# Attention in 256-query strips with the score matmuls in groups of 12, on one Trainium2 core

## The chip, the cores and the metric

The kernel runs on 1 core of one Trainium2 chip. The metric is the device time of one execution in microseconds (us). Executions of one kernel agree within about 0.3%; each was run several times and the median is quoted. Where a ratio is given, it compares the fast runs of two kernels of the same rounds, with a 95% interval, so it is not quite the ratio of the medians.

Engine names in the profile: PE is TensorE's matmuls, PEld its weight loads, DVE is VectorE, ACT is ScalarE, POOL is GpSimd, SP is SyncE.

## The reference

Attention without a softmax over 8 batches of 3008 positions, then an MLP on the 24064 rows:

```python
scores = (1.0 / S) * np.matmul(z, z.transpose(0, 2, 1))   # z: (8, 3008, 64)
attn = np.maximum(scores, 0.0) ** 2
x = (u * np.matmul(attn, v)).reshape(B * S, D)            # u, v: (8, 3008, 256)
h = x @ w_in                                              # (256, 2048)
out = (h * (1.0 / (1.0 + np.exp(-1.702 * h)))) @ w_out    # (2048, 256)
```

## The kernel before

The sequence is padded to 24 blocks of 128. The contraction of a score matmul is only 64 long, so the kernel keeps `z` transposed twice in `ZT`: in partitions 0 to 63 and again in 64 to 127. Two score matmuls (two blocks of keys) can then use the two halves of the array's rows at once (in the trace below they start 3 ns apart). Each strip of 512 queries runs over 12 pairs of key blocks ("units"):

```python
ISUP = 512                                   # queries in a strip
ps_sc: bufs=2, each [128, 2, 512] f32        # 2 score tiles = 4 PSUM banks
ps_o:  bufs=2, each [128, 4, 256] f32        # 2 outputs O  = 4 PSUM banks
...
for gk in range(B * NIT + DPIPE):            # one unit per turn
    ... # casts of V for the next batch, alternating VectorE and ScalarE
    for g in range(2):                       # 2 score matmuls, one per half of the rows
        j = 2 * jp + g
        h0 = g * DQK                         # DQK = 64
        pe.matmul(sc[:, g, :], ZT[h0:h0 + DQK, j * P:(j + 1) * P],
                  ZT[h0:h0 + DQK, isup * ISUP:(isup + 1) * ISUP], start=True, stop=True)
    # unit gk - 1: r = relu(sc), every 5th on VectorE, else on ScalarE
    # unit gk - 1: ap_ = r * r, every 4th on GpSimd, else on VectorE
    # unit gk - 6: 8 value matmuls of 256 columns, O += ap_.T @ V16
    ...
    # end of a strip: X = O * ru on VectorE (ru holds the rows of u)
```

The second copy of `z` in `ZT` is made by a DMA from the first. The order of the instructions on every engine is chosen by the framework's scheduler. `X` goes to DRAM (`xdram`) and comes back transposed (`XT`) for the MLP stage, which the change does not touch.

## Time and profile before

| | before |
|---|---|
| time, median | 1516.7 us |
| first value matmul | 35.2 us |
| last value matmul | 821.5 us |
| one unit in the steady stage | 1.302 us |
| batches 2 to 6, each | 96.7 to 98.9 us |

A batch is measured from its first score matmul to the next batch's (for the last one, to the last value matmul). The times of the table come from the start times in the trace.

The page first: busy time and share of the span, then the chain of work that ended last.

```profile
PE 1449.0 (96%) x10464; PEld 916.0 (61%) x10464; DVE 1124.2 (74%) x1117; ACT 891.2 (59%) x869; POOL 284.7 (19%) x152
...
PE 73%; DVE 2%; ACT 1%; issue 1%; DMA 0%; SPq 0%; ACTq 0%
PE hg L299 23%; PE yps L324 22%; PE O L260 21%; PE sc L225 7%; ACT r L239 1%; DVE X L269 0%; DVE r L237 0%; DMA xdram<-X 0%; PE ztp L132 0%; DVE V_4421 L188 0%; DVE GT L307 0%; DVE V_5575 L188 0%; ACT tsg L306 0%; ACT V_6729 L190 0%; DVE ap__7938 L245 0%
```

TensorE bounds the kernel. But a busy PE is not a PE at its peak, because the ends of matmuls in the profile are modelled: value matmuls are recorded with 272 ns each and start 109 ns apart. The timeline of PE (start in us, duration, engine, line, operation, tiles, shapes, count) shows the steady stage:

```profile
416.34 0.39 PE L225 MATMUL sc<-ZT 64*128 64x512 f16 x2
416.66 1.05 PE L260 MATMUL O<-V_2113,ap__4472 128*128 128x256 f16 x8
417.64 0.39 PE L225 MATMUL sc<-ZT 64*128 64x512 f16 x2
417.96 1.05 PE L260 MATMUL O<-V_2113,ap__4488 128*128 128x256 f16 x8
```

From one pair of scores to the next is 1.30 us. `64*128` on the score lines is the part of the array in use: 64 active rows of the 128 that the value matmuls show. The start times of the single instructions show what the 1.30 us hold (start in us, engine, tile):

```
416.133 PE    O<-V,ap     last of 8 value matmuls, these start 109 ns apart
416.333 PEld  <-ZT        200 ns later: 109 of streaming, 91 of nothing
416.338 PE    sc<-ZT      half 0 of the rows
416.341 PE    sc<-ZT      half 1 of the rows, 3 ns later
416.655 PEld  <-ap        314 ns later: 216 of streaming, 98 of nothing
416.659 PE    O<-V,ap     first of the next 8
```

The 216 ns are what matmuls of 512 columns take elsewhere in this trace: those of the MLP stage start 215 to 216 ns apart. (The prediction below took about 213, and so 101 for the second gap.) So 8 x 109 ns of value matmuls, one stream of 216 ns for both scores, and about 0.2 us in which nothing streams, for each of 576 units.

Last, what PE waited for (us in total, times, longest), and the windows view of the undisturbed middle of attention. Its columns are: stretch, length, then for PE, PEld, DVE, ACT and POOL the busy time with the number of instructions, the granted clock, the DMA share and GB/s.

```profile
PE sc L225 <- DMA ZT<-ZT: 17.0, 1, 17.0
PE ztp L132 <- DVE zst_90 L110: 11.2, 1, 11.2
PE sc L225 <- DVE r L237: 10.6, 11, 2.4
PE hg L299 <- DVE GT L307: 8.7, 2, 7.9
PE sc L225 <- ACT r L239: 5.7, 5, 4.1
```

```profile
core 0: us, PE busy (x) PEld busy (x) DVE busy (x) ACT busy (x) POOL busy (x), PEclk, DMA share, GB/s
200.00:700.00 500.00, 490.12 (x3816) 302.69 (x3815) 389.22 (x405) 323.88 (x313) 179.25 (x92) 1.00 0.26 74
```

The first scores wait 17 us for the DMA that makes the second copy of `z`; after that there is little waiting. VectorE is busy 389 of 500 us, 78%.

### The profile page before, as it was taken

How to read it: one execution, taken by the hardware profiler on the slowest of the kernel's cores; microseconds unless marked ns; L12 is line 12 of the kernel's file. 1: busy time of each engine (PE TensorE's matmuls, PEld its weight loads, DVE VectorE, ACT ScalarE, POOL GpSimd, SP SyncE). 2: the span in 40 equal slices, each digit the busy share in tenths (PEclk: the TensorE clock that was granted, in tenths of full speed). 3: DMA queues.
4: the chain of work that ended last, by engine and by line, in shares of the span. 5: the costliest groups of instructions: out<-in, count | busy, mean ns of one | idle time of the engine just before them, and what ended most of it. 6: DMA issues, size and time to landing. Idle time of an engine off the chain costs nothing.

```text
span 1513.0 us, 24662 instructions
## 1 busy us (share of the span) xinstructions
PE 1449.0 (96%) x10464; PEld 916.0 (61%) x10464; DVE 1124.2 (74%) x1117; ACT 891.2 (59%) x869; POOL 284.7 (19%) x152
## 2 busy tenths in 40 slices
PE   2999999999999999999997999999999999999998
PEld 1565565665656666666665566666666666666666
DVE  3877678778777777777775877777777777777775
ACT  2765566666666676666664665555555655655553
POOL 0333333333333333333432000000000000000000
PEclk9999999999999999999999999999999999999999
DMA  9924325025142121211201112112111121121111
GB/s 307 261 70 115 96 58 164 29 58 164 48 132 67 42 70 34 82 33 43 78 29 54 36 56 64 49 57 59 51 59 49 57 63 49 56 63 50 57 44 48
DMA packets 175422, 113.66 MB, mean 75 GB/s; under 512 B 77776, under 2 KB 174032, under 8 KB 175056
## 3 DMA queue, kind: packets, MB, share of 16 engines
q1 hardware_dynamic: 123376, 95.56, 21.4%
q10 hardware_dynamic: 51136, 12.33, 3.8%
q0 software_dynamic: 800, 4.19, 0.8%
q8 instruction: 82, 1.34, 0.4%
q14 instruction: 28, 0.23, 0.1%
HBM read 59.64 MB, written 36.96 MB: 64 GB/s over the span
## 4 chain that ended last, share of the span: by engine, by line
PE 73%; DVE 2%; ACT 1%; issue 1%; DMA 0%; SPq 0%; ACTq 0%
PE hg L299 23%; PE yps L324 22%; PE O L260 21%; PE sc L225 7%; ACT r L239 1%; DVE X L269 0%; DVE r L237 0%; DMA xdram<-X 0%; PE ztp L132 0%; DVE V_4421 L188 0%; DVE GT L307 0%; DVE V_5575 L188 0%; ACT tsg L306 0%; ACT V_6729 L190 0%; DVE ap__7938 L245 0%
## 5 line engine op out<-in xcount | busy, mean ns | idle before, releaser
L239 ACT ACTIVATE r<-sc 128x1024 f16<-128x1024 f32 x461 | 468.9, 1022 | 278.7 <-PE sc L225 264.1
L306 ACT ACTIVATE tsg<-hg 128x1024 f16<-128x1024 f32 x376 | 379.7, 1023 | 286.0 <-PE hg L299 181.4
L307 DVE TENSOR_TENSOR GT<-hg,tsg 128x1024 f16<-128x1024 f32 x376 | 447.1, 1221 | 113.8 <-ACT tsg L306 111.5
L299 PE MATMUL hg<-XT,W_63 128*128 128x512 f16 x1504 | 372.0, 380 | 10.1 <-DVE GT L307 8.7
L324 PE MATMUL yps<-W_64,GT 128*128 128x256 f16 x3008 | 374.1, 273 | 0.0
L324 PEld LDWEIGHTS <-GT 128*128 128x128 f16 x3008 | 294.2, 98 | 94.0
L225 PE MATMUL sc<-ZT 64*128 64x512 f16 x1152 | 228.5, 389 | 33.8 <-DMA ZT<-ZT 17.0
L299 PEld LDWEIGHTS <-W_63 128*128 128x128 f16 x1504 | 146.4, 97 | 151.9 <-issue 27.1
L237 DVE TENSOR_SCALAR r<-sc 128x1024 f16<-128x1024 f32 x115 | 139.9, 1216 | 17.3 <-PE sc L225 17.2
L225 PEld LDWEIGHTS <-ZT 64*128 64x128 f16 x1152 | 57.4, 93 | 155.5 <-issue 135.8
L330 DVE TENSOR_SCALAR ysb<-yps 128x512 f32<-128x512 f32 x94 | 64.5, 686 | 64.4 <-PE yps L324 64.4
L269 DVE TENSOR_TENSOR X<-O,ru 128x1024 f16<-128x1024 f32 x48 | 58.4, 1218 | 4.8 <-PE O L260 4.8
L139 ACT ACTIVATE ZT<-ztp 64x1536 f16<-64x1536 f16 x16 | 23.0, 1443 | 25.7 <-PE ztp L132 25.7
L132 PE MATMUL ztp<-ident,zst_90 128*64 128x128 f16 x24 | 2.8, 314 | 11.2 <-DVE zst_90 L110 11.2
L132 PEld LDWEIGHTS <-zst_90 128*64 128x64 f16 x24 | 2.5, 174 | 11.2 <-DVE zst_90 L110 11.2
L306 ACT ACT_TABLE_LOAD x1 | 1.3, 1283 | 13.5 <-DMA xdram<-X 13.5
L158 DVE CAST V_96<-vst 128x1536 f16<-128x1536 f32 x4 | 3.6, 954 | 7.0 <-DMA vst<-in_v_dram 7.0
L110 DVE CAST zst_90<-zst 128x1536 f16<-128x1536 f32 x1 | 1.0, 960 | 9.0 <-DMA zst<-in_z_dram 9.0
L243 POOL TENSOR_TENSOR ap__186<-r 128x1024 f16<-128x1024 f16 x1 | 1.9, 1887 | 21.6 <-ACT r L239 21.6
L110 DVE CAST zst_136<-zst 128x1536 f16<-128x1536 f32 x1 | 1.0, 960 | 5.9 <-DMA zst<-in_z_dram 5.9
L245 DVE TENSOR_TENSOR ap__1480<-r 128x1024 f16<-128x1024 f16 x1 | 0.7, 692 | 4.8 <-ACT r L239 4.8
L243 POOL TENSOR_TENSOR ap__1510<-r 128x1024 f16<-128x1024 f16 x1 | 1.9, 1892 | 11.7 <-ACT r L239 11.7
(1773 smaller groups left out, 1774.3 us busy)
## 6 DMA issues: line engine op xcount, KB each, us to landing
out_dram<-ysb SPq DMA_DIRECT2D x47, 512.0 KB, 2.9
vst<-in_v_dram SPq DMA_DIRECT2D x8, 2944.0 KB, 13.1
ru<-in_u_dram SPq DMA_DIRECT2D x40, 512.0 KB, 3.9
xdram<-X SPq DMA_DIRECT2D x8, 1472.0 KB, 7.1
zst<-in_z_dram SPq DMA_DIRECT2D x8, 736.0 KB, 6.2
ZT<-ZT SPq DMA_DIRECT2D x8, 384.0 KB, 3.8
ru<-in_u_dram SPq DMA_DIRECT2D x8, 384.0 KB, 3.5
w1s<-in_moe_w_in_dram POOLq DMA_DIRECT2D x1, 2048.0 KB, 10.5
```

The costliest lines, as they stand in the source:

```text
L132: pe.transpose(ztp[:DQK, jj, :], zst16[:, j, :], ident)
L139: act.activation(zts[b][:DQK, g * (NJ // 2) * P:(g + 1) * (NJ // 2) * P], ztp[:DQK], AF.Copy, scale=1.0)
L225: pe.matmul(sc[:, g, :], ZT[h0:h0 + DQK, j * P:(j + 1) * P], ZT[h0:h0 + DQK, isup * ISUP:(isup + 1) * ISUP], start=True, stop=True,)
L237: dve.tensor_scalar(r[:, :, :], sc[:, :, :], 0.0, csc, ALU.max, ALU.mult)
L239: act.activation(r[:, :, :], sc[:, :, :], AF.Relu, scale=csc)
L260: pe.matmul(O[:, ib, :], ap_[:, g, ib * P:(ib + 1) * P], V16[:, j, :], start=first, stop=last,)
L269: dve.tensor_tensor(X[:, isup * NIBS:(isup + 1) * NIBS, :], O, ru, ALU.mult)
L299: pe.matmul(hg[:, e, :TBC], W1[:, k, ff * P:(ff + 1) * P], XT[:, k, :TBC], start=(k == 0), stop=(k == NK - 1),)
L306: act.activation(tsg[:, :, :TBC], hg[:, :, :TBC], AF.Sigmoid, scale=1.702 / FSC)
L307: dve.tensor_tensor(GT[:, fg * FFG:(fg + 1) * FFG, :TBC], hg[:, :, :TBC], tsg[:, :, :TBC], ALU.mult,)
L324: pe.matmul(yps[:, s2, :], GT[:, ff, s * P:(s + 1) * P], W2[:, ff, :], start=(ff == 0), stop=(ff == NFF - 1),)
L330: dve.tensor_scalar(ysb[:, yy * 2:yy * 2 + ns2, :], yps[:, :ns2, :], 1.0 / FSC, None, ALU.mult)
```

## The change

The intent is fewer turns between half-row score matmuls and full-row value matmuls. Strips become 256 queries, so that an output `O` takes 512 f32 a partition, one PSUM bank in the unit in which the pools above are counted, instead of two. The two banks that this saves make a third score tile: six banks for scores, three tiles of two banks, each holding 4 score matmuls of 256 columns. Three units form a group: 12 score matmuls, then the value matmuls of the group two before. PE runs in the written order. `z` is cast twice, side by side, so that one transpose on PE writes both copies. All casts of V move to VectorE, and the casts of the MLP's weights move from the start into batch 0. Small things change too: there are more buffers for the squares and for `ru`, and the zeros for the padding are written by GpSimd instead of VectorE.

The diff, cut to its core, with some lines joined:

```diff
+    ISUP = 256
+    UNITS = NJ // 4
+    GRP = 3
+    LAG = 2 * GRP
...
-        tc.tile_pool(name="ps_sc", bufs=2, space=bass.MemoryType.PSUM) as ps_sc,
+        tc.tile_pool(name="ps_sc", bufs=3, space=bass.MemoryType.PSUM) as ps_sc,
         tc.tile_pool(name="ps_o", bufs=2, space=bass.MemoryType.PSUM) as ps_o,
+        tc.manual_schedule(engines={mybir.EngineType.PE}),
...
-            zst16 = pa.tile([P, NJ, DQK], F16, name="zst16", tag="zst16")
-            dve.tensor_copy(zst16, zst)
+            zst16 = pa.tile([P, NJ, 2, DQK], F16, name="zst16", tag="zst16")
+            for h in range(2):
+                js = slice(h * half, (h + 1) * half)
+                for c in range(2):
+                    dve.tensor_copy(zst16[:, js, c, :], zst[:, js, :])
...
-                pe.transpose(ztp[:DQK, jj, :], zst16[:, j, :], ident)
+                pe.transpose(ztp[:, jj, :], zst16[:, g * ZG + jj, :, :], ident)
-            sp.dma_start(zts[b][DQK:2 * DQK, :], zts[b][:DQK, :])
...
+            sc = ps_sc.tile([P, 2, 2, ISUP], F32, name="sc", tag="sc")
+            for p in range(2):
+                for r_ in range(2):
+                    j = 4 * q + 2 * p + r_
+                    h0 = r_ * DQK
+                    pe.matmul(sc[:, r_, p, :], ZT[h0:h0 + DQK, j * P:(j + 1) * P],
+                        ZT[h0:h0 + DQK, isup * ISUP:(isup + 1) * ISUP],
+                        start=(p == 0), stop=(p == 1))
...
+            for g in range(0, B * NU + LAG, GRP):
+                    if k == 12 and b == 0:
+                            dve.tensor_copy(W1, w1s)
+                            dve.tensor_copy(W2, w2s)
+                        if k in (12, 18, 24, 30, 36, 42):
+                            v_cast(b + 1)
+                        if k in (48, 54, 60):
+                            zt_part(b + 1, (k - 48) // 6)
+                    for t in range(g, g + GRP):
+                        scores(t)
+                if g >= LAG:
+                    for t in range(g - LAG, g - LAG + GRP):
+                        attend(t)
```

In the built order PE runs 12 scores and 24 value matmuls in turn (the 48 of the change's description counts the weight loads too). The split of the relus and squares among the engines stays: every 5th relu on VectorE, every 4th square on GpSimd.

More of the change, by code (lines that the diff above doesn't have):

```diff
@@ L88, in load_xt @@
             )
+    ISUP = 256
+    NIS = SPAD // ISUP
+    NIBS = ISUP // P
+    UNITS = NJ // 4
+    NU = NIS * UNITS
+    GRP = 3
+    LAG = 2 * GRP
+    ZG = 8
     with (
@@ L93, with load_batch @@
         tc.tile_pool(name="pr", bufs=7) as pr,
-        tc.tile_pool(name="ps_sc", bufs=2, space=bass.MemoryType.PSUM) as ps_sc,
+        tc.tile_pool(name="ps_sc", bufs=3, space=bass.MemoryType.PSUM) as ps_sc,
         tc.tile_pool(name="ps_o", bufs=2, space=bass.MemoryType.PSUM) as ps_o,
+        tc.manual_schedule(engines={mybir.EngineType.PE}),
     ):
-        tcount = 0
         loads = {}
         zts = {}
-        def emit_loads(b):
+        Xd = {}
+        def load_batch(b):
             if b >= B:
@@ L104, in emit_loads @@
             zst = pa1.tile([P, NJ, DQK], F32, name="zst", tag="zst")
-            sp.dma_start(zst[:, :NJ - 1, :], z[b, :S0].rearrange("(n p) d -> p n d", p=P))
+            vst = pa1.tile([P, NJ, D], F32, name="vst", tag="vst")
+            if SREM:
+                pool.memset(zst[SREM:, NJ - 1, :], 0.0)
+                pool.memset(vst[SREM:, NJ - 1, :], 0.0)
+            half = NJ // 2
+            zd = z[b, :S0].rearrange("(n p) d -> p n d", p=P)
+            sp.dma_start(zst[:, :half, :], zd[:, :half, :])
+            sp.dma_start(zst[:, half:NJ - 1, :], zd[:, half:, :])
             if SREM:
                 sp.dma_start(zst[:SREM, NJ - 1, :], z[b, S0:S].unsqueeze(1))
-                dve.memset(zst[SREM:, NJ - 1, :], 0.0)
-            zst16 = pa.tile([P, NJ, DQK], F16, name="zst16", tag="zst16")
-            dve.tensor_copy(zst16, zst)
-            vst = pa1.tile([P, NJ, D], F32, name="vst", tag="vst")
             sp.dma_start(vst[:, :NJ - 1, :], v[b, :S0].rearrange("(n p) c -> p n c", p=P))
@@ L114, in emit_loads @@
                 sp.dma_start(vst[:SREM, NJ - 1, :], v[b, S0:S].unsqueeze(1))
-                dve.memset(vst[SREM:, NJ - 1, :], 0.0)
+            zst16 = pa.tile([P, NJ, 2, DQK], F16, name="zst16", tag="zst16")
[3 more added lines that the diff above has]
+                    dve.tensor_copy(zst16[:, js, c, :], zst[:, js, :])
             V16 = pa.tile([P, NJ, D], F16, name="V16", tag="V16", bufs=3)
             X = pa.tile([P, NJ, D], F16, name="X", tag="X")
-            casts = [(V16[:, 6 * q:6 * (q + 1), :], vst[:, 6 * q:6 * (q + 1), :]) for q in range(4)]
@@ L119, in emit_loads @@
-            loads[b] = (zst16, V16, X, casts)
-        ztbuf = {}
-        def emit_zt_tr(b, g):
-            if b >= B:
-                return
-            zst16 = loads[b][0]
-            if b not in zts:
-                zts[b] = pa.tile([P, SPAD], F16, name="ZT", tag="ZT")
-            ztp = ps_o.tile([P, NJ // 2, P], F16, name="ztp", tag="O")
-            for jj in range(NJ // 2):
-                j = g * (NJ // 2) + jj
-                pe.transpose(ztp[:DQK, jj, :], zst16[:, j, :], ident)
-            ztbuf[(b, g)] = ztp
@@ L135, in emit_zt_ev @@
-        def emit_zt_ev(b, g):
-            if b >= B:
-                return
-            ztp = ztbuf.pop((b, g))
-            act.activation(zts[b][:DQK, g * (NJ // 2) * P:(g + 1) * (NJ // 2) * P], ztp[:DQK], AF.Copy, scale=1.0)
-        def emit_zt_dup(b):
-            if b >= B:
-                return
-            sp.dma_start(zts[b][DQK:2 * DQK, :], zts[b][:DQK, :])
-        def emit_zt(b):
-            emit_zt_tr(b, 0)
-            emit_zt_ev(b, 0)
-            emit_zt_tr(b, 1)
-            emit_zt_ev(b, 1)
-            emit_zt_dup(b)
@@ L153, with zt_part @@
-        DPIPE = 6
-        NIT = NIS * NJP
-        PRO_AT = NIT * 3 // 4
-        emit_loads(0)
-        for _o, _i in loads[0][3]:
-            dve.tensor_copy(_o, _i)
-        loads[0][3].clear()
-        emit_zt(0)
-        emit_loads(1)
+            zts[b] = pa.tile([P, SPAD], F16, name="ZT", tag="ZT")
+            casts = [(V16[:, 4 * q:4 * (q + 1), :], vst[:, 4 * q:4 * (q + 1), :]) for q in range(NJ // 4)]
+            loads[b] = (zst16, V16, casts)
+            Xd[b] = X
+        def zt_part(b, g):
+            zst16 = loads[b][0]
+            ztp = ps_o.tile([P, ZG, P], F16, name="ztp", tag="O")
+            for jj in range(ZG):
+                pe.transpose(ztp[:, jj, :], zst16[:, g * ZG + jj, :, :], ident)
+            act.activation(zts[b][:, g * ZG * P:(g + 1) * ZG * P], ztp, AF.Copy, scale=1.0)
@@ new lines, in v_cast, with load_u @@
+        def v_cast(b):
+            casts = loads[b][2]
+            if casts:
+                o, i_ = casts.pop(0)
+                dve.tensor_copy(o, i_)
+        def load_u(b, isup):
+            ru = pa.tile([P, NIBS, D], F32, name="ru", tag="ru", bufs=4)
+            lo = isup * ISUP
+            hi = min(S, lo + ISUP)
+            nfull = (hi - lo) // P
+            sp.dma_start(
+                ru[:, :nfull, :],
+                u[b, lo:lo + nfull * P].rearrange("(n p) c -> p n c", p=P),
+            )
+            rem = (hi - lo) - nfull * P
+            if rem > 0:
+                sp.dma_start(ru[:rem, nfull, :], u[b, lo + nfull * P:hi].unsqueeze(1))
+                pool.memset(ru[rem:, nfull, :], 0.0)
+            return ru
@@ new lines, with scores @@
+        aps = {}
+        Os = {}
+        us = {}
+        def scores(t):
+            b, k = divmod(t, NU)
+            isup, q = divmod(k, UNITS)
+            ZT = zts[b]
+            if q == 0:
+                us[(b, isup)] = load_u(b, isup)
+            sc = ps_sc.tile([P, 2, 2, ISUP], F32, name="sc", tag="sc")
[3 more added lines that the diff above has]
+                    h0 = r_ * DQK
+                    pe.matmul(
+                        sc[:, r_, p, :],
+                        ZT[h0:h0 + DQK, j * P:(j + 1) * P],
+                        ZT[h0:h0 + DQK, isup * ISUP:(isup + 1) * ISUP],
+                        start=(p == 0), stop=(p == 1),
+                    )
+            r = pr.tile([P, 2, 2, ISUP], F16, name="r", tag="r")
+            if (t + 1) % DVE_RELU_EVERY == 0:
+                dve.tensor_scalar(r, sc, 0.0, csc, ALU.max, ALU.mult)
+            else:
+                act.activation(r, sc, AF.Relu, scale=csc)
+            ap_ = pr.tile([P, 2, 2, ISUP], F16, name="ap_", tag="ap_", bufs=11)
+            aps[t] = ap_
+            if (t + 1) % POOL_SQ_EVERY == 0:
+                pool.tensor_tensor(ap_, r, r, ALU.mult)
+            else:
+                dve.tensor_tensor(ap_, r, r, ALU.mult)
@@ new lines, in attend @@
+        def attend(t):
+            b, k = divmod(t, NU)
+            isup, q = divmod(k, UNITS)
+            ap_ = aps.pop(t)
+            V16 = loads[b][1]
+            if q == 0:
+                Os[isup] = ps_o.tile([P, NIBS, D], F32, name="O", tag="O")
+            O = Os[isup]
+            for p in range(2):
+                for r_ in range(2):
+                    j = 4 * q + 2 * p + r_
+                    for ib in range(NIBS):
+                        pe.matmul(
+                            O[:, ib, :],
+                            ap_[:, r_, p, ib * P:(ib + 1) * P],
+                            V16[:, j, :],
+                            start=(j == 0 and ib == 0), stop=(j == NJ - 1 and ib == NIBS - 1),
+                        )
+            if q == UNITS - 1:
+                X = Xd[b]
+                ru = us.pop((b, isup))
+                dve.tensor_tensor(X[:, isup * NIBS:(isup + 1) * NIBS, :], O, ru, ALU.mult)
+                del Os[isup]
+                if isup == NIS - 1:
+                    sp.dma_start(
+                        xdram[b * S:b * S + S0].rearrange("(n p) c -> p n c", p=P),
+                        X[:, :NJ - 1, :],
+                    )
+                    if SREM:
+                        sp.dma_start(xdram[b * S + S0:(b + 1) * S].unsqueeze(1), X[:SREM, NJ - 1, :])
@@ L162 @@
+        load_batch(0)
+        for g in range(NJ // ZG):
+            zt_part(0, g)
+        load_batch(1)
         with tc.tile_pool(name="wstage", bufs=1) as wstage:
@@ L164 @@
             pool.dma_start(w1s, moe_w_in.rearrange("(ko p) f -> p ko f", p=P))
-            dve.tensor_copy(W1, w1s)
             w2s = wstage.tile([P, NFF, D], F32, name="w2s", tag="ws")
             pool.dma_start(w2s, moe_w_out.rearrange("(fo p) c -> p fo c", p=P))
-            dve.tensor_copy(W2, w2s)
-        ZT_TR0 = 42
-        ZT_EV0 = 44
-        ZT_TR1 = 55
-        ZT_EV1 = 57
-        ZT_DUP = 58
-        V16d = {}
-        Xd = {}
-        scs = {}
-        aps = {}
-        Os = {}
@@ L179 @@
-        us = {}
-        for gk in range(B * NIT + DPIPE):
-            b0, k0 = divmod(gk, NIT)
-            if b0 < B:
-                if k0 == 0:
-                    _, V16d[b0], Xd[b0], _c = loads.pop(b0)
-                if k0 % 4 == 2 and (b0 + 1) in loads and loads[b0 + 1][3]:
-                    o, i_ = loads[b0 + 1][3].pop(0)
-                    if (k0 // 4) % 2 == 0:
-                        dve.tensor_copy(o, i_)
-                    else:
-                        act.activation(o, i_, AF.Copy, scale=1.0)
-                if k0 == PRO_AT:
-                    emit_loads(b0 + 2)
-                if k0 == ZT_TR0:
-                    emit_zt_tr(b0 + 1, 0)
-                elif k0 == ZT_EV0:
-                    emit_zt_ev(b0 + 1, 0)
-                elif k0 == ZT_TR1:
-                    emit_zt_tr(b0 + 1, 1)
-                elif k0 == ZT_EV1:
-                    emit_zt_ev(b0 + 1, 1)
-                elif k0 == ZT_DUP:
-                    emit_zt_dup(b0 + 1)
-                isup, jp = divmod(k0, NJP)
-                ZT = zts[b0]
-                if jp == 0:
-                    ru = pa.tile([P, NIBS, D], F32, name="ru", tag="ru")
-                    us[(b0, isup)] = ru
-                    lo = isup * ISUP
-                    hi = min(S, lo + ISUP)
-                    nfull = (hi - lo) // P
-                    if nfull:
-                        sp.dma_start(
-                            ru[:, :nfull, :],
-                            u[b0, lo:lo + nfull * P].rearrange("(n p) c -> p n c", p=P),
-                        )
-                    rem = (hi - lo) - nfull * P
-                    if rem > 0:
-                        sp.dma_start(ru[:rem, nfull, :], u[b0, lo + nfull * P:hi].unsqueeze(1))
-                        dve.memset(ru[rem:, nfull, :], 0.0)
-                sc = ps_sc.tile([P, 2, ISUP], F32, name="sc", tag="sc")
-                scs[gk] = sc
-                for g in range(2):
-                    j = 2 * jp + g
-                    h0 = g * DQK
-                    pe.matmul(
-                        sc[:, g, :],
-                        ZT[h0:h0 + DQK, j * P:(j + 1) * P],
-                        ZT[h0:h0 + DQK, isup * ISUP:(isup + 1) * ISUP],
-                        start=True, stop=True,
-                    )
-            g1 = gk - 1
-            if g1 >= 0 and g1 in scs:
-                sc = scs.pop(g1)
-                r = pr.tile([P, 2, ISUP], F16, name="r", tag="r")
-                tcount += 1
-                if DVE_RELU_EVERY and tcount % DVE_RELU_EVERY == 0:
-                    dve.tensor_scalar(r[:, :, :], sc[:, :, :], 0.0, csc, ALU.max, ALU.mult)
-                else:
-                    act.activation(r[:, :, :], sc[:, :, :], AF.Relu, scale=csc)
-                ap_ = pr.tile([P, 2, ISUP], F16, name="ap_", tag="ap_")
-                aps[g1] = ap_
-                if POOL_SQ_EVERY and tcount % POOL_SQ_EVERY == 0:
-                    pool.tensor_tensor(ap_, r, r, ALU.mult)
-                else:
-                    dve.tensor_tensor(ap_, r, r, ALU.mult)
-            g2 = gk - DPIPE
-            if g2 >= 0 and g2 in aps:
-                b2, k2 = divmod(g2, NIT)
-                isup, jp = divmod(k2, NJP)
-                ap_ = aps.pop(g2)
-                V16 = V16d[b2]
-                if jp == 0:
-                    Os[(b2, isup)] = ps_o.tile([P, NIBS, D], F32, name="O", tag="O")
-                O = Os[(b2, isup)]
-                for g in range(2):
-                    j = 2 * jp + g
-                    for ib in range(NIBS):
-                        first = (jp == 0 and g == 0 and (ib % 2) == 0)
-                        last = (jp == NJP - 1 and g == 1 and (ib % 2) == 1)
-                        pe.matmul(
-                            O[:, ib, :],
-                            ap_[:, g, ib * P:(ib + 1) * P],
-                            V16[:, j, :],
-                            start=first, stop=last,
-                        )
-                if jp == NJP - 1:
-                    X = Xd[b2]
-                    ru = us.pop((b2, isup))
-                    dve.tensor_tensor(X[:, isup * NIBS:(isup + 1) * NIBS, :], O, ru, ALU.mult)
-                    del Os[(b2, isup)]
-                    if isup == NIS - 1:
-                        sp.dma_start(
-                            xdram[b2 * S:b2 * S + S0].rearrange("(n p) c -> p n c", p=P),
-                            X[:, :NJ - 1, :],
-                        )
-                        if SREM:
-                            sp.dma_start(xdram[b2 * S + S0:(b2 + 1) * S].unsqueeze(1), X[:SREM, NJ - 1, :])
-                        del Xd[b2], V16d[b2], zts[b2]
@@ new lines @@
+            for g in range(0, B * NU + LAG, GRP):
+                b, k = divmod(g, NU)
+                if b < B:
+                    if g < NU:
+                        while loads[0][2]:
+                            v_cast(0)
+                    if k == 12:
+                        if b == 0:
+                            dve.tensor_copy(W1, w1s)
+                            dve.tensor_copy(W2, w2s)
+                    if b + 1 < B:
+                        if k in (12, 18, 24, 30, 36, 42):
+                            v_cast(b + 1)
+                        if k in (48, 54, 60):
+                            zt_part(b + 1, (k - 48) // 6)
+                    if k == 66:
+                        load_batch(b + 2)
+                    for t in range(g, g + GRP):
[3 more added lines that the diff above has]
+                        attend(t)
```

## The prediction

> **What bounds the kernel now.** TensorE. The page gives PE 96% busy of 1513 us; the chain of waits is 73% PE (value matmuls 21%, scores 7%, MLP 45%). The MLP stage, 691 us from 822 us on, is not touched. Attention runs from the first real score at 32 us to 822 us.
>
> In the timeline one steady unit (2 score matmuls of 512 columns, 8 value matmuls of 256) takes 1.30 us. Value matmuls follow each other every 109 ns: 872. The two scores start 3 ns apart, on two halves of the rows, and cost one stream of about 213. The rest, 215 ns, is mainly two gaps: 91 ns before the scores' weight loads, 101 after them. [...] 576 x 0.215 = 124 us on the critical path. After 60 us the waits list gives PE only 18 us.
>
> **What the change does.**
> - In the built order PE runs 12 scores, then 24 value matmuls (48 counts their weight loads), 192 times: 384 switches replace 1150.
> - Scores become 2304 matmuls of 256 columns, 6 pairs per group: same streaming (6 x 110 = 660 ns), if each half's next weights load while it streams. At the trace's start a second score of the same half did start when the first had streamed, its weights loaded early, but at 512 columns.
> - Group: 24 x 109 + 660 + 215 = 3.49 us, against 3.90 for three units before. 192 groups: 670 us against 750.
> - z duplicated on PE removes the DMA copy ZT<-ZT, for which the first scores waited 17 us. First value matmul near 23 us instead of 35.
> - VectorE gets more: all V casts (6 x 0.65 us a batch), z cast twice, 96 X evictions of 512 columns instead of 48 of 1024 (estimate 0.66 us), and the weight casts (2 x 2.3 us) move from the idle start into attention.
>
> **VectorE becomes the second limit.** Per batch: relu 14.4 x 1.217 = 17.5; squares 54 x 0.933 = 50.4 (0.69 undisturbed; GpSimd's squares hold up many); X 7.9; V 4.5; z 2.2: 82.5 us. PE needs 24 x 3.49 + 1.7 (transposes) = 85.5. VectorE would be 96% busy, with relus that PE waits for in its queue, so I expect 88 to 90 us a batch instead of 98.
>
> **Sum.** 22 (start) + 8 x 89 + 8 (weight casts, drain) = 742 us for the end of attention, 80 before 822. 1516 - 80 = 1436.
>
> Predicted: 1436 us; 8 in 10 between 1408 and 1478. Faster by over 2%: 0.86; within 2%: 0.12; slower: 0.02.
>
> **What would show each step.** Timeline of PE: score pairs 110 ns apart, one gap of 100 ns on either side, group 3.5 us. PE's waits: scores waiting for the relu on VectorE, tens of us in total. Windows: VectorE over 90% in attention (77% before), MLP stage the same 691 us.
>
> **What would make it wrong.** If weights of the same half cannot load behind a 256-column stream, a pair takes 200 ns and a group 4.05 us: no gain but the start. If VectorE keeps up, 1410. If its queue stalls PE in each burst (a burst fills all six score banks; three relus on ScalarE take 3.07 of 3.49 us), a batch could take 95 us: 1485.

215 ns and 576 x 0.215 = 124 us are from the trace. The second score at the trace's start came 402 ns after the first, its weight load 11 ns after it. The 200 ns a pair at the end is an estimate; a stream of 109 ns and a weight load of 93 (the mean of the scores' in the kernel before) make 202.

## The result, and the profile after

| | before | after |
|---|---|---|
| time, median | 1516.7 us | 1457.5 us |
| ratio | | 0.960 (95%: 0.9585 to 0.9619) |
| first value matmul | 35.2 us | 21.9 us |
| last value matmul | 821.5 us | 765.7 us |
| three units in the steady stage | 3.906 us | 3.487 us |
| batch 0, batch 1 | 114.2, 105.8 us | 110.0, 101.1 us |
| batches 2 to 6, each | 96.7 to 98.9 us | 88.5 to 91.9 us |

The page, the same parts:

```profile
PE 1380.4 (95%) x11616; PEld 996.3 (68%) x11616; DVE 1177.3 (81%) x1195; ACT 847.4 (58%) x863; POOL 305.1 (21%) x176
...
PE 79%; DVE 11%; DMA 4%; issue 3%; ACT 2%; ACTq 1%; SPq 0%; DVEq 0%
PE O L213 26%; PE hg L284 24%; PE yps L309 22%; PE sc L183 7%; DVE r L191 2%; DMA vst<-in_v_dram 2%; ACT r L193 1%; DVE X L222 1%; DMA xdram<-X 1%; ACTq L85 1%; DMA zst<-in_z_dram 1%; DVE V_1333 L151 0%; DVE zst_7973 L132 0%; DVE V_6649 L151 0%; DVE V_3991 L151 0%
```

VectorE's share of the chain went from 2% to 11%. The timeline of PE in a steady group:

```profile
304.93 0.83 PE L183 MATMUL sc<-ZT 64*128 64x256 f16 x12
305.69 1.05 PE L213 MATMUL O<-V_1333,ap__3816 128*128 128x256 f16 x8
306.57 1.04 PE L213 MATMUL O<-V_1333,ap__3825 128*128 128x256 f16 x8
307.45 1.04 PE L213 MATMUL O<-V_1333,ap__3834 128*128 128x256 f16 x8
308.42 0.83 PE L183 MATMUL sc<-ZT 64*128 64x256 f16 x12
```

3.49 us for what took 3 x 1.30. In the single start times the six pairs of scores follow each other every 109 ns, two matmuls 3 ns apart in each; there is one gap before them and one after. What PE waited for, and the middle of attention:

```profile
PE sc L183 <- DVE r L191: 24.2, 10, 4.8
PE O L213 <- DVE X L222: 15.7, 16, 1.6
PE ztp L144 <- DVE zst_97 L132: 10.5, 2, 5.6
PE hg L284 <- DVE GT L292: 9.5, 2, 8.8
PE sc L183 <- ACT r L193: 8.3, 6, 6.4
```

```profile
200.00:700.00 500.00, 476.49 (x4914) 379.65 (x4912) 450.65 (x486) 322.02 (x336) 205.84 (x111) 0.99 0.27 77
```

The wait for the copy of `z` is gone. PE now waits for VectorE, which is 90% busy here.

A stop of PE can cost more than its length. The windows view around one stop:

```profile
322.00:326.40 4.40, 4.40 (x48) 3.31 (x47) 4.40 (x4) 2.06 (x3) 2.81 (x2) 1.00 0.22 63
326.50:329.10 2.60, 0.00 (x0) 0.00 (x0) 2.60 (x4) 1.72 (x2) 0.28 (x1) 1.00 1.02 290
330.20:333.60 3.40, 3.40 (x18) 2.36 (x17) 3.08 (x6) 0.43 (x1) 0.74 (x2) 0.50 0.49 130
334.00:337.40 3.40, 3.40 (x38) 2.70 (x36) 3.40 (x5) 1.94 (x2) 1.06 (x1) 1.00 0.95 327
```

PE does nothing for 2.6 us, and then, from 330.2 us on, its clock (the third column from the right) is 0.50 for 3.4 us. The timeline of PE shows the same stop and eight value matmuls taking nearly twice as long:

```profile
329.12 0.39 PE L183 MATMUL sc<-ZT 64*128 64x256 f16 x4 [2.66 <-DVE r L191]
329.44 1.22 PE L213 MATMUL O<-V_2662,ap__4163 128*128 128x256 f16 x8
330.46 1.91 PE L213 MATMUL O<-V_2662,ap__4172 128*128 128x256 f16 x8
```

Not every stop does this. Stops of 2.0 us (238.7 to 240.8) and 2.7 us (326.5 to 329.1) in the changed kernel were followed by 3.4 us of half clock, while another of 2.0 us there (421.4 to 423.4) and one of 2.4 us in the kernel before (344.8 to 347.3) were not. What decides this, the traces do not show. Up to 760 us the clock record (it begins at 29.8 us in the changed kernel and at 39.4 in the one before) has 37.5 us at half clock in the changed kernel and 6.8 in the one before. At half clock value matmuls start 213 ns apart in place of 109, so this extra half clock cost at most about 15 us, half of 37.5 - 6.8 (an estimate).

The account of attention, with the two steady periods:

| us | before | after | difference |
|---|---|---|---|
| first value matmul | 35.2 | 21.9 | -13 |
| steady periods (576 x 1.302; 192 x 3.487) | 750.0 | 669.5 | -80 |
| the rest, up to the last value matmul | 36 | 74 | +38 |
| last value matmul | 821.5 | 765.7 | -56 |

The last row is the sum of the three; the rest holds the transposes, the waits and the half clock. So the change wins 93 us and gives 38 back. The experiments ask two things: is the steady gain really the number of turns, and what are the 38 us?

### The profile page after: what moved, and what is told of

Its sections match the earlier page's. It is cut to its first block, busy times and chain, and to the rows that moved or that the text cites. A ratio compares the mean times of both kernels' runs of the same rounds, so it can differ in the third digit from the quotient of the medians.

```text
span 1456.5 us, 27175 instructions
## 1 busy us (share of the span) xinstructions
PE 1380.4 (95%) x11616; PEld 996.3 (68%) x11616; DVE 1177.3 (81%) x1195; ACT 847.4 (58%) x863; POOL 305.1 (21%) x176
## 4 chain that ended last, share of the span: by engine, by line
PE 79%; DVE 11%; DMA 4%; issue 3%; ACT 2%; ACTq 1%; SPq 0%; DVEq 0%
PE O L213 26%; PE hg L284 24%; PE yps L309 22%; PE sc L183 7%; DVE r L191 2%; DMA vst<-in_v_dram 2%; ACT r L193 1%; DVE X L222 1%; DMA xdram<-X 1%; ACTq L85 1%; DMA zst<-in_z_dram 1%; DVE V_1333 L151 0%; DVE zst_7973 L132 0%; DVE V_6649 L151 0%; DVE V_3991 L151 0%
## 5 line engine op out<-in xcount | busy, mean ns | idle before, releaser
L193 ACT ACTIVATE r<-sc 128x1024 f16<-128x1024 f32 x461 | 443.1, 1024 | 256.1 <-PE sc L183 237.0
L183 PE MATMUL sc<-ZT 64*128 64x256 f16 x2304 | 165.0, 275 | 32.5 <-DVE r L191 24.2
L183 PEld LDWEIGHTS <-ZT 64*128 64x128 f16 x2304 | 98.5, 95 | 83.1 <-issue 71.5
L222 DVE TENSOR_TENSOR X<-O,ru 128x512 f16<-128x512 f32 x96 | 65.3, 680 | 6.8 <-PE O L213 6.8
L145 ACT ACTIVATE ZT<-ztp 128x1024 f16<-128x1024 f16 x24 | 24.4, 1023 | 36.2 <-PE ztp L144 36.2
L291 ACT ACT_TABLE_LOAD x1 | 1.3, 1283 | 14.2 <-DMA xdram<-X 14.2
L151 DVE CAST V_1333<-vst 128x1024 f16<-128x1024 f32 x6 | 5.6, 966 | 0.9 <-DMA vst<-in_v_dram 0.9
L151 DVE CAST V_102<-vst 128x1024 f16<-128x1024 f32 x6 | 3.8, 689 | 2.9 <-DMA vst<-in_v_dram 2.9
L151 DVE CAST V_5320<-vst 128x1024 f16<-128x1024 f32 x6 | 5.6, 962 | 0.0
```

The lines of the kernel that those rows point to most:

```text
L145: act.activation(zts[b][:, g * ZG * P:(g + 1) * ZG * P], ztp, AF.Copy, scale=1.0)
L151: dve.tensor_copy(o, i_)
L183: pe.matmul(sc[:, r_, p, :], ZT[h0:h0 + DQK, j * P:(j + 1) * P], ZT[h0:h0 + DQK, isup * ISUP:(isup + 1) * ISUP], start=(p == 0), stop=(p = ...
L193: act.activation(r, sc, AF.Relu, scale=csc)
L222: dve.tensor_tensor(X[:, isup * NIBS:(isup + 1) * NIBS, :], O, ru, ALU.mult)
L291: act.activation(tsg[:, :, :TBC], hg[:, :, :TBC], AF.Sigmoid, scale=1.702 / FSC)
```

## The experiments

### Is it the turns? Groups of one and of two

Theory A: the steady gain is fewer changes of tiling mode (here the turn between half-row and full-row matmuls). Rival B: it is the third score tile, the written order and the shorter start.

```diff
-    GRP = 3
-    LAG = 2 * GRP
+    GRP = 1
+    LAG = 6
```

> The changed kernel with one unit per group (4 scores, 8 value matmuls), everything else kept: three score tiles, PE in written order, 256-query strips, lag of 6 units. Theory A (the gain is fewer changes of tiling mode, about 215 ns for each pair of them): one unit takes 8 x 109 + 2 x 110 + 215 = 1305 ns, 3.91 us for three, so attention is 192 x 0.43 = 82 us longer, less some 20 us because VectorE gets slack: 1505 to 1535 us, about the time of the kernel before. Rival B (the gain is the third score tile, the written order and the shorter start, not the number of switches): it stays below 1475.

Measured: 1501.4 us, ratio to before 0.989 (0.988 to 0.991). The median unit takes 1.303 us, just the 1.302 of the kernel before, with its order, its third score tile and its short start all kept. Rival B had it below 1475 us and falls. The time is 4 us below Theory A's range: as expected some stalls went, but more of them (the sum over the median period is 40 us in place of 78).

With `GRP = 2`:

> The same with two units per group (8 scores, 16 value matmuls): 288 pairs of switches instead of 192. Theory A: two units take 2.40 us, 1.20 a unit against 1.16; 96 x 0.215 = 21 us more, less a few for slack on VectorE: 1465 to 1480 us. Rival B: the same as the changed kernel within noise.

Measured: 1463.8 us, ratio to before 0.965 (0.963 to 0.967); two units take 2.397 us. It is 1 us below the range, for the same reason. The three sizes lie on a line: 1.303, 2.397, 3.487 us, that is 1.092 us for each unit and 0.21 us for each pair of turns. The single start times of the kernel before give nearly the same: 91 + 98 ns of nothing, and the second value matmul of a run comes 120 instead of 109 ns after the first.

The pair is also a warning. From groups of two to groups of three the steady period wins 96 x 0.21 = 20 us, but the measured gain is 1463.8 - 1457.5 = 6 us. The larger the group, the more is given back.

### Without a change of mode, does the group matter?

Here the scores use all 128 rows. `ZT` holds `z` twice, so this gives twice the score, and the factor in the relu is halved; the result is right. Nothing in attention then uses half the rows, but two scores no longer share a stream.

```diff
-                        ZT[h0:h0 + DQK, j * P:(j + 1) * P],
-                        ZT[h0:h0 + DQK, isup * ISUP:(isup + 1) * ISUP],
+                        ZT[:, j * P:(j + 1) * P],
+                        ZT[:, isup * ISUP:(isup + 1) * ISUP],
...
-                dve.tensor_scalar(r, sc, 0.0, csc, ALU.max, ALU.mult)
+                dve.tensor_scalar(r, sc, 0.0, csc / 2, ALU.max, ALU.mult)
-                act.activation(r, sc, AF.Relu, scale=csc)
+                act.activation(r, sc, AF.Relu, scale=csc / 2)
```

> The changed kernel with each score matmul contracted over all 128 rows (z stands there twice, so twice the score; the factor in relu is halved, the result is right). No matmul of attention then uses half the rows. Theory A: the gaps around the runs of scores vanish (scores and value matmuls all 109 ns apart), but the pairs no longer share a stream: 36 x 109 = 3.92 us a group, 83 us more in attention, less 20 us of stalls: 1510 to 1535 us. If the gaps stay at about 100 ns each, they are not the mode but something else at the turn (a wait, the PSUM banks): 4.1 us a group, about 1560.

Measured: 1508.7 us, ratio to before 0.995 (0.993 to 0.997), 1 us under the range. The timeline of PE of this kernel:

```profile
590.21 1.47 PE L182 MATMUL sc<-ZT 128*128 128x256 f16 x12
591.52 1.04 PE L212 MATMUL O<-V,ap__7571 128*128 128x256 f16 x8
592.39 1.04 PE L212 MATMUL O<-V,ap__7580 128*128 128x256 f16 x8
```

The first value matmul starts 1.31 us after the first score: 12 x 109 ns, so there is no gap at the turn. The group takes 3.93 us. With groups of one as well:

> Both edits: one unit per group and scores over all 128 rows. Theory A: with no change of mode the size of the group does not matter: within 1% of the run with 128 rows and groups of three, 1305 to 1310 ns a unit. If a turn between scores and values costs something whatever the mode, it is 384 x 0.2 = 80 us slower than that run.

Measured: 1506.2 us, ratio 0.993 (0.991 to 0.994); one unit takes 1.310 us, a third of 3.930. With no change of mode the size of the group does not matter, although scores and values alternate just as often. So the gap comes with the change between half-row and full-row matmuls, 0.21 us for a change there and back. What TensorE does in it, the traces do not show.

### Where the 38 us went: VectorE's load?

Theory C: VectorE's mean load delays relus and X. Rival D: it is the burst, a group filling all six score banks at once with three relus in a row on ScalarE. First, less load:

```diff
-DVE_RELU_EVERY = 5
+DVE_RELU_EVERY = 9
```

> The changed kernel with every 9th instead of every 5th relu on VectorE: 8 a batch instead of 14.4, so VectorE is relieved of 6.4 x 1.21 = 7.8 us a batch and ScalarE gets 6.6 more; PE's work is the same. Theory C (the gain that went missing, some 78 us over the steady period of 3.487 us a group, is VectorE's load: relus late in its queue, X late): PE's waits for VectorE fall by half, batches 2 to 7 go from 90 us to 87, total 1430 to 1445 us. Rival D (it is the burst itself: a group fills all six score banks and its three relus on ScalarE take 3.07 of 3.49 us): now more groups have all three relus on ScalarE, so no gain or a loss, 1455 to 1475 us, with waits for the relu on ScalarE in place of VectorE's.

Measured: 1443.5 us, ratio to before 0.952 (0.951 to 0.954), in Theory C's range, and Rival D's longer time did not come. PE's waits for VectorE, whole run:

```profile
PE sc L183 <- DVE r L191: 24.7, 13, 5.4
PE O L213 <- DVE X L222: 3.4, 7, 0.5
```

The wait for X fell from 15.7 to 3.4 us, but the wait for relus did not fall (24.2 before this edit). Together they fell from 39.9 to 28.1 us, not by half. Between 200 and 700 us, 12.5 us of waits for relus remain, and the batches 2 to 6 fell only to 85.6 to 90.7 us. Less load helps; something else holds VectorE.

### Casts in a row?

The scheduler put the six casts of V of a batch close together on VectorE: in the steady batches within 7 to 9 us, up to four in a row, with squares and relus between (the text below says four to six in a row; the trace shows no such row). The four longest stops of PE between 200 and 700 us (at 238.7, 326.5, 421.4 and 510.5 us) all fall among such casts. Theory E: casts in a row are what stops PE.

```diff
-        tc.manual_schedule(engines={mybir.EngineType.PE}),
+        tc.manual_schedule(engines={mybir.EngineType.PE, mybir.EngineType.DVE}),
```

> VectorE too runs in the written order, so the six V casts of a batch stand one in every second group instead of four to six in a row as the scheduler put them. VectorE's work is the same. Theory E (what costs is not VectorE's mean load but casts in a row, which delay a relu past the three score tiles, and the half clock of TensorE after such a stop): the long stops in groups 3 to 5 of each batch go, 15 to 25 us less, 1433 to 1443 us. If the mean load is what counts: within 6 us of the changed kernel. If VectorE in written order waits for relus and loads instead: slower.

Measured: 1483.4 us, ratio 0.978 (0.976 to 0.980): slower than the changed kernel. The casts were spread, but PE waited more:

```profile
PE sc L183 <- DVE r L191: 57.8, 35, 15.1
```

The third of the outcomes that were named came: in the written order VectorE waits for loads and relus itself (the first value matmul came at 36.0 us, and the waits for loads include 10.2 us for the second MLP weight). Theory E gets no support, but the run changed too much at once to refute it for the scheduler's order. A later run (no squares on GpSimd) comes closer to that.

### The stop in batch 1

The waits of ScalarE in the changed kernel hold one long one:

```profile
ACT r L193 <- DMA XT<-xdram: 11.8, 1, 11.8
```

The loads of `XT` for the MLP stage are issued from ScalarE's queue, the scheduler put the first ones into batch 1, and there they stand in front of the relus until `xdram` is written. The kernel before has the same wait with 8.4 us.

```diff
-        load_xt(0, act)
+        load_xt(0, sp)
...
-                load_xt(tb + 1, act)
+                load_xt(tb + 1, sp)
```

> The transposing loads XT<-xdram are issued from SyncE's queue instead of ScalarE's. In the changed kernel (and in the one before, 8 us there) ScalarE's queue stood 11.8 us in batch 1 behind the first of them, which waited for xdram; a half clock followed. Expected: that stop goes, batch 1 falls from 101 to about 90 us: 1443 to 1449 us; more if the start of the MLP stage, where ScalarE waits 14 us for xdram, gains too. If the loads of u and v now stand behind the transposes in SyncE's queue, some of it comes back as waits for V casts or X.

Measured: 1447.1 us, ratio 0.954 (0.953 to 0.956), as expected. Batch 1 takes 92.9 us in place of 101.1. (The half clock of that stop, in the changed kernel, lasted 10.2 us, from 145.9 us on; it began within the stop.) The start of the MLP stage gained nothing: the wait of 14.2 us for `xdram` stayed.

### The weight casts in batch 0

```diff
             pool.dma_start(w1s, moe_w_in.rearrange("(ko p) f -> p ko f", p=P))
+            dve.tensor_copy(W1, w1s)
...
                         if b == 0:
-                            dve.tensor_copy(W1, w1s)
                             dve.tensor_copy(W2, w2s)
```

> The cast of the first MLP weight goes back to the start, as in the kernel before, so the second weight's load starts early too and its cast need not wait for it. Batch 0 took 110 us from the first score, 20 over batch 2. If the weight casts in attention are what makes it long: about 5 us less (2.85 us of cast, 2.4 us of wait, part of the half clock), 1450 to 1455 us. If the load of the second weight only takes bandwidth from v and z at the start: same as the changed kernel.

Measured: 1454.7 us, ratio 0.960 (0.958 to 0.961). That is the edge of the first range, but the interval overlaps that of the changed kernel (0.9585 to 0.9619), which was timed in other rounds: some 3 us, not told apart from nothing. The first value matmul came later (24.5 us) and batch 0 was shorter (107.4 us).

### GpSimd's squares

The squares on VectorE took 1.03 us on average between 210 and 700 us in the changed kernel, with a median of 0.68. The timeline shows where the long ones are:

```profile
459.49 0.68 DVE L199 TENSOR_TENSOR ap__6190<-r 128x1024 f16<-128x1024 f16 x1
...
460.38 1.89 POOL L197 TENSOR_TENSOR ap__6199<-r 128x1024 f16<-128x1024 f16 x1 [2.57 <-ACT r L193]
...
461.26 1.57 DVE L199 TENSOR_TENSOR ap__6208<-r 128x1024 f16<-128x1024 f16 x1 [1.09 <-ACT r L193]
```

GpSimd's square ends at 460.38 + 1.89 = 462.27. VectorE's square, begun at 461.26, ends at 462.83, 0.56 us after that. An undisturbed square takes 0.68 us, so it got about 0.12 us of its work done in the 1.01 us until GpSimd was through. This is no single case: of 293 squares on VectorE between 210 and 700 us, 79 took over 0.8 us (1.28 to 2.38), and every one of them ended 0.55 us after a GpSimd square that had begun before it. They hold 102 us of VectorE's time more than undisturbed squares would. So a good fifth of VectorE's "busy" time in this stretch is being held, not work. Not every instruction of VectorE is held: X and the relus, which read PSUM, take 0.68 and 1.21 us throughout, also the 16 and 38 of them that ran over 0.2 us beside a GpSimd square. (A few casts of V and z were held too, up to 2.38 and 2.25 us in place of 0.68 and 0.55.) What the two engines contend for, the traces do not show. What if no square runs on GpSimd, at the price of 18 more a batch on VectorE?

```diff
-POOL_SQ_EVERY = 4
+POOL_SQ_EVERY = 1 << 30
```

> The changed kernel with no square on GpSimd: VectorE does all 72 of a batch. Squares on VectorE took 1.03 us on average in the changed kernel's batches 2 to 7 (0.93 in the kernel before), 0.68 where GpSimd was not running. If GpSimd's squares only hold VectorE up: 72 x 0.68 = 49 us a batch in place of 54 x 1.03 = 55.6, and V and z casts 1 to 2 us less, so VectorE is relieved by about 8 us a batch, as with fewer relus: 1435 to 1447 us, no square over 0.75 us. If the slow squares are slow for another reason, VectorE gets 18 x 1.03 = 18.5 us more a batch and is the bottleneck: over 1490 us.

Measured: 1419.1 us, ratio to before 0.936 (0.935 to 0.938): 38 us less than the changed kernel, where 10 to 22 were expected. The squares take 0.69 us on average. Batches 2 to 6 take 85.0 to 86.0 us, where 24 x 3.487 us and some 1.3 us of transposes make 85.0. The windows view of the stretch from 200 to 700 us, first of the run with fewer relus on VectorE:

```profile
200.00:700.00 500.00, 485.08 (x5032) 386.55 (x5032) 408.69 (x460) 362.10 (x379) 202.71 (x114) 1.00 0.27 78
```

and of the run without squares on GpSimd, with all the waits of PE in that stretch after it:

```profile
200.00:700.00 500.00, 498.85 (x5198) 398.49 (x5196) 432.37 (x616) 338.75 (x355) 2.75 (x10) 1.00 0.28 79
```

```profile
PE sc L183 <- DVE r L191: 1.3, 3, 0.7
```

This refutes Theory C as it was put. VectorE is busier here (432 us) than with fewer relus (409 us), and yet PE is busy 499 us and waits 1.3 us, where it waited 15 there. What stops PE is not VectorE's mean load but GpSimd's share of the squares. The likely way is the collisions: single squares of 1.3 to 2.4 us in a queue in which a relu has to be done within a group. Rival D falls too as a cause of its own: the bursts against the six banks are all still there. So does Theory E: the six casts of V still come within 8 to 10 us, up to three in a row. Casts and bursts may still have mattered together with the hold-ups.

What this run does not separate: it removes the hold-ups of VectorE, and with them the long squares on GpSimd itself (1.9 us at least, up to 2.9), whose results PE also needs; and the scheduler's order on VectorE changed somewhat. The waits lists of the changed kernel speak for the hold-ups: in attention PE never waits for a GpSimd square directly, and ScalarE does for 3.5 us in all.

### Did the kernel before pay this too?

The same line changed in the kernel before:

> The kernel before with no square on GpSimd. There TensorE had only about 18 us of waits after 60 us, and VectorE was 77% busy with GpSimd's squares. If GpSimd's squares became a cost through the change (bursts, less slack), it gains little here: 1498 to 1514 us. If they cost the kernel before as much as the changed one (38 us), they are no part of where the gain went: 1475 to 1485 us. Slower than 1520 if VectorE or its queue gets too long.

Measured: 1505.1 us, ratio 0.993 (0.991 to 0.995): 11 us. So GpSimd's squares cost the kernel before 11 us and the changed one 38; 27 us of this cost came with the change. Two things changed there that were not told apart: VectorE has less slack (without GpSimd's squares it is busy 86% in place of 77% between 200 and 700 us), and the collisions are longer, though not more: between 210 and 700 us, 79 squares were held for 1.29 us each, in place of 87 for 0.76 each. With no squares on GpSimd in both kernels, the change is worth 1505.1 - 1419.1 = 86 us, and the account is close to what the streaming promises:

| us, no squares on GpSimd | before | after | difference |
|---|---|---|---|
| first value matmul | 35.1 | 22.2 | -13 |
| steady periods | 750.0 | 669.5 | -80 |
| the rest | 26 | 34 | +8 |
| last value matmul | 811.2 | 725.4 | -86 |

### Together

Every 9th relu on VectorE, no square on GpSimd, `XT` from SyncE:

> The reliefs together: every 9th relu on VectorE, no square on GpSimd, transposing loads from SyncE. By theory C (VectorE's load, and ScalarE's stop in batch 1) they add up as far as there are stalls left to remove: batches 2 to 7 near 86 us (24 x 3.487 + 1.3 of transposes + a little), batch 1 near 88, total 1420 to 1432 us. If stalls come from the burst against the six score banks, batches stay at 88 to 90 us and the total at 1435 to 1445.

Measured: 1413.1 us, ratio 0.933 (0.931 to 0.934), under the range by 7 us. Batches 1 to 5 take 85.8 to 86.2 us. With GpSimd's squares gone, moving relus off VectorE has nothing left to win: batches 2 to 5 are even 0.2 to 1.2 us longer than without it. The last run therefore keeps the relu split of the change and adds the early weight cast:

> The changed kernel with no square on GpSimd, transposing loads from SyncE, first weight's cast at the start, and the relu split of the change (every 5th on VectorE). Batches 1 to 7 at 85 to 86 us (24 x 3.487 + 1.3), batch 0 near 100: 1404 to 1412 us. If the earlier load of the second weight or the loads on SyncE cost something here, about 1413, no better than with the three reliefs.

Measured: 1408.3 us, ratio to before 0.929 (0.928 to 0.931), in the expected range. Batches 1 to 6 take 85.0 to 86.2 us as expected; batch 7, counted to the last value matmul, takes 88.7, over it. It beats both kernels: 108 us under the one before and 49 under the changed one.

## Why the prediction was right or wrong

The measured 1457.5 us lies in the range (1408 to 1478), 21 us above the predicted 1436.

- "576 x 0.215 = 124 us on the critical path": right. Three group sizes give 0.21 us a pair of turns, and with no change of mode neither the gap nor the effect of the group is there.
- "Group: ... 3.49 us": right, 3.487. The worry that weights of the same half would not load behind a stream of 256 columns was unfounded: the second pair's loads start 11 ns after the first pair's matmuls, and the six pairs start 109 ns apart.
- "First value matmul near 23 us": right, 21.9.
- "VectorE over 90% in attention": right by the count, 450.65 of 500 us are 90%, but 102 us of this is squares held by GpSimd.
- "MLP stage the same 691 us": right; 1456.5 - 765.8 us from its first matmul is 690.7.
- "8 x 89 + 8": this is the term that was too small. From first to last value matmul it should have been 720 us and was 743.8. Batches 2 to 7 took 541 us instead of 534; the first two, from the first value matmul, took 202.5 us instead of 186. Two causes were not in the sum. One is ScalarE's queue, stopped 11.8 us in batch 1 by a load of `XT`, though the kernel before already showed that wait with 8.4 us; moving the load gave 10 us. The other is the half clock in or after many of the longer stops: 37.5 us of it in place of 6.8. With 3.4 us at half clock after it, a stop of 2.0 us costs about 3.7 (an estimate: 2.0 and half of 3.4). Which part of the 24 us belongs to the clock alone was not tested.
- "VectorE becomes the second limit. ... VectorE would be 96% busy, with relus that PE waits for in its queue": the wait was there, 24.2 us, but the reason was not the mean load. The prediction had the number in hand (squares of 0.933 us, 0.69 undisturbed, because GpSimd holds many up) and used it only as a mean, which rose to 1.03 us in the changed kernel. Taking GpSimd's squares away gave back 38 us with VectorE at 432 of 500 us, more than with fewer relus, where PE still waited. So that the steady batches came out at 88.5 to 91.9 us, close to the predicted 88 to 90, is partly luck: the size was argued from a mean load that is not the cause.

## What to carry to other kernels

Count the turns between half-row and full-row matmuls: at the 0.21 us measured here for a change there and back, grouping won in proportion to the turns that it removed (1.303, 2.397 and 3.487 us for groups of one, two and three units). The rest depends on the other engines' keeping up with the bursts: with VectorE held by GpSimd 38 us of the gain were given back here, without that 8. When a gain on the bounding engine comes out smaller than its period says, look at the helpers for single long instructions, not only for mean load: here a second engine that was given work to help VectorE held it up, and taking the help away was worth as much as two thirds of the change itself. Some stops of TensorE here (2.0 and 2.7 us) were followed by 3.4 us at half clock, so removing a rare long stop can be worth more than its length (not tested apart from its cause here).
